# Middle of a 2-D FFT's row transform, woven into matmuls: its groups ordered by pairs of column halves

## The chip, the cores and the metric

The kernel runs on one core of a Trainium2 chip. The time is that of one execution on the device in microseconds (us); the median of several runs counts. The engines are TensorE (PE; its weight loads are shown as PEld), VectorE (DVE), ScalarE (ACT), GpSimd (POOL) and SyncE (SP). Each works through its own queue in order, and they wait for each other by semaphores. Transfers are issued by the queues of SP, ACT and POOL.

## The reference, cut to what is computed

```python
x = A_x                                              # 2048 x 1024, bf16
g = sigmoid((x * gate_w).sum(-1, keepdims=True))
a = irfft2(rfft2(x) * (w_r + 1j * w_i))              # over both axes, Df = 513
r = relu(B_x @ w1 + b1); b = (r * r) @ w2 + b2       # 1024 -> 3584 -> 1024
out = g * a + (1 - g) * b
# returned: out, and the gradients for A_x, w_r, w_i, w1, b1, w2, b2, gate_w
```

The gradients need the same transform of the incoming gradient, the product of both spectra (for w_r and w_i), and the way back.

## The kernel before, in words

**Main and side work.** The MLP is the main work: long chains of 128x128 matmuls on PE. First come `units` (`mlp_in`, up to about 456 us: chains `ph`, `pZ` and `pd`, four or eight matmuls each, L783 and L884), then `grads` (`mlp_grads`: `pX`, `pV`, L1206, up to about 850 us), then the outputs. The Fourier part is side work: generators that yield after each step. `spread` takes a number of side steps, given by a rate, between two pieces of the main work: 1.5 per piece while the middle of the transform runs beside `units` (one and two in turn; a unit is four pieces), 1.2 per piece beside `grads`, where most pieces count half, and from `res1` on what is left over 44 pieces (`todo`, L1870). So the Fourier part lies between main chains on every engine.

**Who sets the order.** The program's text gives the priority. A planner with estimated times then orders each engine's queue, and an instruction that it takes to be ready earlier may overtake. `behind` and `after(..., NoSync)` pin an order by hand. A tile is a buffer with a tag; `bufs` says how many such buffers there are, and whoever writes one anew waits for its last reader. In main work the wait that matters is on PSUM banks: ACT copies `cu` and `u` (L888), ACT's Relu (L898) and DVE's sum `rT` (L900) must have read a bank before PE goes on in it.

**The middle of the row transform** (`fft_mid`). The 2048 rows are 32 x 64. The first stage has left, for each of the 32 outputs c of a 32-point transform, 64 rows of complex numbers, for x and for the gradient, in `z_scr`. The middle takes c and 16 + c together as m = 0..15 (`NM`), and the columns in two halves: first h = 1, then h = 0. A pair of halves belongs to one m. For each (m, h), 32 in all:

- `inputs`: z is loaded (two transfers; from the third on issued by ACT, L404);
- `mirrored` (L425, m > 0): DVE makes pm, the sum and the difference of z's two parts;
- `transform`: px, four matmuls of 128 x 64 (L435), two for each half of the partitions, into a PSUM tile of tag `ps2`; ACT casts it into x (L436), writes a negated part (L437) and the edges (L438);
- `by_groups`: POOL lays out the filter w; `filters` (POOL's DMAs) loads filter and matrices of the next m;
- `products` (DVE, tt, two of L446) and `joined` (y, L451, L454, L458; eh by ACT, L455, L456): the filtered spectrum;
- `back`: pv, four matmuls of 64 x 128 (L466), into the other tile of `ps2`; ACT copies half of it (vc, L471), DVE makes pc (L472, L473), POOL stores it to `y_scr` (L475);
- `grads_of_w` (DVE, g and gs, L485, L486; g shares a buffer with tt) and `grads_out` (ACT, gw, L490, L495; POOL stores, L499): the gradient of the filter.

`ps2` has two buffers, so two tiles of px or pv are in use at a time. In the kernel before, the 32 halves are turns of four steps: step 1 px of this half and its x; step 2 pm of the next half, then pv and pc of the half before, then tt; step 3 y; step 4 gw of the half before, g and gs of this one. So px of one half and pv of another alternate, one step apart, at 4 steps a half.

`fft_out`, the last stage, loads `y_scr` after the middle has ended and begins its work 14 steps later.

Of the kernel before, what the change touches and what calls it, by code (L numbers as in the profile page):

```python
# [10 lines left out]
P = 128  # L11
BF16 = mybir.dt.bfloat16
FP16 = mybir.dt.float16
FP32 = mybir.dt.float32
ALU = mybir.AluOpType
ACT = mybir.ActivationFunctionType

FDT = FP16
# [123 lines left out]
def kernel(  # L142
# [22 lines left out]
    nc = tc.nc  # L165
# [8 lines left out]
    R1, R2 = g.R1, g.R2  # L174
    NT = S // P
    Q, H, LW, W1 = D // 4, D // 2, g.Df + 1, g.Df
# [8 lines left out]
    V, mm = nc.vector.tensor_tensor, nc.tensor.matmul  # L185
# [15 lines left out]
    pers, _ = pool("pers", stack=ctx)  # L201
    dram, _ = pool("dram", space=DRAM, stack=ctx)
# [25 lines left out]
    HW, HL = H // 2, P // 2  # L228
# [31 lines left out]
    def behind(ins, eng):  # L260
        after(ins, ahead[eng], mybir.DependencyClass.NoSync)
# [71 lines left out]
    def fft_mid(filler):  # L333
# [15 lines left out]

        def edges_through(ams):  # L350
            flat = lambda t_: t_[:].rearrange("p a b l -> p (a b l)")
            parted = fb.tile([P, 2, 2, HW], FDT, name="parted", tag="pm")
            parted = flat(parted)[:, 0 : 4 * P].rearrange("p (e k i) -> p e k i", e=4, i=NT)
            of_edge = edge[:].rearrange("p x t i -> p (x t) i").unsqueeze(2).to_broadcast([P, 4, 8, NT])
            of_part = part_of[:].unsqueeze(1).unsqueeze(3).to_broadcast([P, 4, 8, NT])
            tied = lambda ins: after(ins, later["last"], mybir.DependencyClass.NoSync)
            tied(V(out=parted, in0=of_edge, in1=of_part, op=ALU.mult))
            pe = fps.tile([P, 4, R1], FP32, name="pe", tag="ps2", bufs=2)
            for e in range(4):
                mm(pe[:, e, :], lhsT=parted[:, e].rearrange("p k i -> p (k i)"), rhs=row_of[:], start=True, stop=True, skip_group_check=True)  # L360
            ed = fb.tile([P, 2, 2, HW], FDT, name="ed", tag="y")
            ed = flat(ed)[:, 0 : NM * 8].rearrange("p (m n e) -> p m n e", n=2, e=4)
            by_row = pe[:].rearrange("p e c -> p c e")
            nc.vector.memset(ed[lanes[1], 0], 0.0)
            for n in range(2):
                tied(nc.vector.tensor_copy(out=ed[lanes[0], n:, n, :], in_=by_row[lanes[0], n:NM]))
                a, b = slice(2 * n, 2 * n + 2), slice(2 - 2 * n, 4 - 2 * n)
                tied(nc.vector.tensor_copy(out=ed[lanes[1], 1:, n, a], in_=by_row[lanes[1], NM + 1 :, a]))
                tied(nc.vector.tensor_scalar(out=ed[lanes[1], 1:, n, b], in0=by_row[lanes[1], NM + 1 :, b], scalar1=-1.0, scalar2=None, op0=ALU.mult))
            tied(nc.vector.tensor_copy(out=ed[lanes[0], 0, 1, :], in_=by_row[lanes[0], NM]))  # L370
            sp = fps.tile([P, NM, 2, 4], FP32, name="sp", tag="ps2", bufs=2)
            for h in range(2):
                for m in range(NM // 2):
                    for n in range(2):
                        mm(
                            sp[:, h * NM // 2 + m, n], lhsT=ams[h][:, m, n, :], rhs=ed[:, h * NM // 2 + m, n, :],
                            start=True, stop=True, skip_group_check=True,
                        )
            ex = fb.tile([P, NM, 3, 2, 2], FDT, name="ex", tag="ex")
            for n in range(2):  # L380
                for c in range(2):
                    nc.vector.tensor_copy(
                        out=ex[lanes[n], :, 1 + c], in_=sp[lanes[c], :, n, :].rearrange("p m (e t) -> p m t e", e=2)
                    )
            nc.scalar.mul(out=ex[:, :, 0], in_=ex[:, :, 2], mul=-1.0)
            return ex
# [32 lines left out]
        def mirrored(m, z, summed=None):  # L419

            if m == 0:
                return z
            pm = fb.tile([P, 2, 2, HW], FDT, name="pm", tag="pm")
            for n, op in enumerate((ALU.add, ALU.subtract)):
                mixed = V(out=pm[:, n], in0=z[:, 0], in1=z[:, 1], op=op)  # L425
                behind(mixed, "DVE")
                after(mixed, summed, mybir.DependencyClass.NoSync)
            return pm

        def transform(m, h, pm, ex):  # L430
            x = fb.tile([P, 3, 2, WL], FDT, name="x", tag="x", bufs=2)
            px = fps.tile([P, 2, 2, HW], FP32, name="px", tag="ps2", bufs=2)
            for c in range(2):
                for n in range(2):
                    behind(mm(px[lanes[n], c], lhsT=mats[m][:, 0, n, lanes[c]], rhs=pm[:, n], start=True, stop=True), "PE")  # L435
            nc.scalar.copy(out=x[:, 1:3, :, 0:HW], in_=px[:])  # L436
            copied = nc.scalar.mul(out=x[:, 0, :, 0:HW], in_=px[:, 1], mul=-1.0)  # L437
            nc.scalar.copy(out=x[:, :, :, h * HW], in_=ex[:, m, :, :, h])  # L438
            return x, copied
# [7 lines left out]
            return tt  # L447

        def joined(h, tt, eh):
            y = fb.tile([P, 2, 2, HW], FDT, name="y", tag="y")  # L450
            V(out=y[:], in0=tt[:, 0, :, :, 0:HW], in1=tt[:, 1, :, :, 0:HW], op=ALU.add)  # L451
            if h:
                en = fb.tile([P, 2, 2], FDT, name="en", tag="en")
                V(out=en[:], in0=tt[:, 0, :, :, HW], in1=tt[:, 1, :, :, HW], op=ALU.add)  # L454
                nc.scalar.mul(out=eh[:, 0], in_=en[:, 1], mul=-1.0)  # L455
                nc.scalar.copy(out=eh[:, 1], in_=en[:, 0])  # L456
            else:
                V(out=y[:, :, :, 0], in0=y[:, :, :, 0], in1=eh[:], op=ALU.add)  # L458
            return y

        def back(m, h, y):
            pc = fb.tile([P, 2, 2, HW], FDT, name="pc", tag="pc", bufs=2)
            pv = fps.tile([P, 2, 2, HW], FP32, name="pv", tag="ps2", bufs=2)
            for c in range(2):
                for n in (1, 0):
                    mm(pv[:, n], lhsT=mats[m][lanes[n], 1, c, :], rhs=y[lanes[n], c], start=c == 0, stop=c == 1)  # L466
            if m == 0:
                done = nc.scalar.copy(out=pc[:], in_=pv[:])
            else:
                vc = fb.tile([P, 2, HW], FP32, name="vc", tag="vc")  # L470
                done = nc.scalar.copy(out=vc[:], in_=pv[:, 1])  # L471
                V(out=pc[:, 0], in0=pv[:, 0], in1=vc[:], op=ALU.add)  # L472
                V(out=pc[:, 1], in0=pv[:, 0], in1=vc[:], op=ALU.subtract)  # L473
            for n, c in enumerate((m, R1 // 2 + m)):
                st(out=columns_of(y_scr, c, h), in_=pc[:, n])  # L475
            return done

        def grads_of_w(h, x):
            W = HW + h
# [20 lines left out]

        wn = {0: filters(0)}
        ams = [some_am(0), some_am(1)]
        turns = [(m, h) for m in range(NM) for h in (1, 0)]
        z = {0: inputs(*turns[0])}
        later["mid"] = True
        for _ in range(7):
            next(filler, None)
# [1 line left out]
        ex = edges_through(ams)  # L509
        for _ in filler:  # L510
            yield
        pm, w = mirrored(0, z.pop(0)), by_groups(1, wn[0])
        held = eh = gw = summed = None
        z[1] = inputs(*turns[1])
        yield
        for u, (m, h) in enumerate(turns):
            if h:
                eh = fb.tile([P, 2, 2], FDT, name="eh", tag="eh")
            x, copied = transform(m, h, pm, ex)
            if u + 2 < len(turns):  # L520
                z[u + 2] = inputs(*turns[u + 2], copied)
            yield
            if u + 1 < len(turns):
                pm = mirrored(turns[u + 1][0], z.pop(u + 1), summed)
            if held:
                done = back(*turns[u - 1], held)
            tt = products(h, x, w)
            if u + 1 < len(turns):
                m2, h2 = turns[u + 1]
                w = by_groups(h2, wn[m2])  # L530
            yield
            held = joined(h, tt, eh)
            yield
            if u:
                grads_out(*turns[u - 1], gs, gw, done)
            gs, summed = grads_of_w(h, x)
            if h:
                gw = fb.tile([P, 2, LW], BF16, name="gw", tag="gw", bufs=2)
                if m + 1 < NM:
                    wn[m + 1] = filters(m + 1)  # L540
            yield
        done = back(*turns[-1], held)
        grads_out(*turns[-1], gs, gw, done)
        yield
        fbs.close()

    def fft_out():
# [1319 lines left out]
        pass  # L1867
    grads = mlp_grads()
    next(grads), next(grads)
    todo = 4 * NT - 11 + 7 + 4 * R1 + 2 + 14 + 4 * NT  # L1870

    def rate():
        if "res1" not in later:
# [44 lines left out]
```

## Time and profile before

| | us |
|---|---|
| median of 3 runs | 1196.31 |
| lowest, highest | 1195.17, 1196.74 |
| the profiled execution, its own time | 1203.86 |
| its span, first to last instruction | 1202.1 |
| PE busy in the span | 1179.5 |
| px and pv first and last seen | 232.3, 596.0 |

The profile shows one execution. Busy time is the sum of what an engine worked; an idle time is put down to what released the engine. The lines are those of kernel.py. Matmuls are pipelined: one of 512 columns is shown as 0.38 us long, while the next starts 0.216 us after it, so their starts tell more than their lengths. Rows of the timeline merge neighbouring instructions of a kind (`x4`); their columns are start, extent, engine, line, operation, tile, array shape and operands. A row of the waits has the total, the number of times and the longest.

### The profile page before, as it was taken

How to read it: one execution, taken by the hardware profiler on the slowest of the kernel's cores; microseconds unless marked ns; L12 is line 12 of the kernel's file. 1: busy time of each engine (PE TensorE's matmuls, PEld its weight loads, DVE VectorE, ACT ScalarE, POOL GpSimd, SP SyncE). 2: the span in 40 equal slices, each digit the busy share in tenths (PEclk: the TensorE clock that was granted, in tenths of full speed). 3: DMA queues.
4: the chain of work that ended last, by engine and by line, in shares of the span. 5: the costliest groups of instructions: out<-in, count | busy, mean ns of one | idle time of the engine just before them, and what ended most of it. 6: DMA issues, size and time to landing. Idle time of an engine off the chain costs nothing.

```text
span 1202.1 us, 19429 instructions
## 1 busy us (share of the span) xinstructions
PE 1179.5 (98%) x7181; PEld 636.1 (53%) x7275; DVE 893.5 (74%) x1598; ACT 535.8 (45%) x961; POOL 375.9 (31%) x618
## 2 busy tenths in 40 slices
PE   8989999999999999999999999999999999999998
PEld 5555555443333444444446899999544444444444
DVE  5878887689898887776637666666786677986757
ACT  5657888576767783444414556564201010000000
POOL 0224433665666663553322322321001100000000
PEclk9999999999999999999999999999999999999999
DMA  9998585686969888989897999994889999665530
GB/s 242 295 237 244 179 210 185 203 200 192 220 189 212 246 243 174 206 183 220 202 225 141 232 218 249 252 208 151 258 170 251 270 255 280 192 188 153 179 123 36
DMA packets 329464, 249.84 MB, mean 208 GB/s; under 512 B 187912, under 2 KB 287658, under 8 KB 328858
## 3 DMA queue, kind: packets, MB, share of 16 engines
q1 hardware_dynamic: 268352, 112.12, 44.8%
q0 software_dynamic: 35136, 111.72, 29.4%
q10 hardware_dynamic: 25882, 24.76, 7.3%
q8 instruction: 57, 0.93, 0.3%
q14 instruction: 37, 0.30, 0.1%
HBM read 114.82 MB, written 89.67 MB: 170 GB/s over the span
## 4 chain that ended last, share of the span: by engine, by line
PE 73%; DVE 12%; DMA 5%; ACT 4%; issue 4%; SPq 1%; POOL 0%; ACTq 0%; another core or an unknown queue 0%; DVEq 0%; POOLq 0%
PE pX L1206 15%; PE xX L1505 13%; PE pV L1206 11%; PE pd L783 8%; PE xV L1505 6%; PE ph L884 6%; PE xZ L1505 3%; DMA dhT_scr<-dhT 1%; PE pui L325 1%; DVE rT L900 1%; PE ph L776 1%; PE pki L591 1%; PE px L435 1%; DVE dhT L787 1%; DMA z<-z_scr 1%
## 5 line engine op out<-in xcount | busy, mean ns | idle before, releaser
L783 PE MATMUL pd<-dbT,w2T 128*128 128x512 bf16 x859 | 205.4, 379 | 4.4 <-DMA w2T<-in_B_w_dram 2.0
L783 PEld LDWEIGHTS <-w2T 128*128 128x128 bf16 x896 | 86.3, 98 | 106.4 <-issue 3.9
L1505 PEld LDWEIGHTS <-dS 128*128 128x128 f16 x686 | 66.3, 98 | 79.1 <-issue 3.4
L787 DVE SCALAR_TENSOR_TENSOR dhT<-pd,rT 128x512 bf16<-128x512 f32 x112 | 76.6, 684 | 32.7 <-PE pd L783 26.0
L1556 POOL DMA_DIRECT2D out_dram<-ot x32 | 17.3, 542 | 249.4 <-DVE ot L1612 128.0
L1622 ACT ACTIVATE w2br<-w2br,dsc 128x512 f32<-128x512 bf16 x8 | 5.8, 722 | 175.0 <-DVE ot L1612 117.4
L1222 ACT COPY u<-pX 128x512 f32<-128x512 f32 x56 | 32.8, 585 | 98.7 <-PE pX L1206 92.6
L1505 PE MATMUL xX<-oT,dS 128*128 128x512 f16 x336 | 76.5, 379 | 0.2 <-DVE eR L1534 0.2
L1505 PEld LDWEIGHTS <-odd 128*128 128x128 bf16 (+1 forms) x462 | 44.8, 98 | 51.5 <-issue 0.9
L1505 PEld LDWEIGHTS <-even 128*128 128x128 bf16 (+1 forms) x448 | 43.6, 98 | 52.6 <-issue 0.7
L1206 PEld LDWEIGHTS <-T 128*128 128x128 f16 x672 | 64.7, 98 | 7.9 <-issue 0.7
L901 ACT ACTIVATE rT<-rT 128x512 bf16<-128x512 bf16 x69 | 43.3, 628 | 40.7 <-DVE rT L900 40.7
L751 ACT ACTIVATE h2T<-rT 128x1024 bf16<-128x1024 bf16 x56 | 59.7, 1065 | 0.5 <-issue 0.2
L1226 DVE TENSOR_TENSOR whi<-pV,u 128x512 bf16<-128x512 f32 x28 | 19.3, 690 | 51.6 <-ACT u L1222 48.1
L475 POOL DMA_DIRECT2D y_scr<-pc x64 | 46.9, 734 | 34.4 <-DVE pc L472 31.9
L446 DVE TENSOR_TENSOR tt<-x,w 128x1028 f16<-128x1028 f16 (+1 forms) x64 | 41.9, 691 | 17.0 <-issue 12.5
L1206 PEld LDWEIGHTS <-S 128*128 128x128 f16 x336 | 32.3, 98 | 41.0 <-DVE S L1138 1.3
L1206 PEld LDWEIGHTS <-resL 128*128 128x128 bf16 x448 | 43.0, 98 | 4.7
L1206 PEld LDWEIGHTS <-resR 128*128 128x128 f16 (+1 forms) x448 | 42.9, 98 | 4.9 <-issue 0.2
L1206 PEld LDWEIGHTS <-even 128*128 128x128 bf16 (+1 forms) x256 | 24.5, 98 | 30.8 <-issue 2.1
L815 POOL DMA_DIRECT2D h2T_scr<-h2T x28 | 20.7, 738 | 62.1 <-ACT f L285 30.8
L499 POOL DMA_DIRECT2D out_dram<-gw x64 | 34.4, 543 | 17.8 <-ACT gw L495 13.9
(381 smaller groups left out, 2757.8 us busy)
## 6 DMA issues: line engine op xcount, KB each, us to landing
h2T_scr<-h2T POOLq DMA_DIRECT2D x28, 512.0 KB, 4.4
dhT_scr<-dhT POOLq DMA_DIRECT2D x28, 512.0 KB, 5.2
y_scr<-pc POOLq DMA_DIRECT2D x64, 128.0 KB, 3.9
ax_scr<-yo POOLq DMA_DIRECT2D x16, 512.0 KB, 5.4
out_dram<-ot POOLq DMA_DIRECT2D x31, 256.0 KB, 3.1
z<-z_scr ACTq DMA_DIRECT2D x60, 128.0 KB, 4.4
out_dram<-whi POOLq DMA_DIRECT2D x28, 256.0 KB, 5.3
out_dram<-wlo POOLq DMA_DIRECT2D x28, 256.0 KB, 5.2
```

Source lines behind the costliest of these rows:

```text
L446: V(out=tt[:, k, :, :, 0:W], in0=x[:, a : a + 2, :, 0:W], in1=by, op=ALU.mult)
L475: st(out=columns_of(y_scr, c, h), in_=pc[:, n])
L499: st(out=every(dst_w, k), in_=gw[lanes[n], c_, 0:W1])
L751: after(nc.scalar.activation(h2T, rT, ACT.Square), behind_, mybir.DependencyClass.NoSync)
L783: mm(pd[:], lhsT=w_[:, ec, fc % FGC * P : (fc % FGC + 1) * P], rhs=dbT[:, ec, ss], start=(ec == 0), stop=(ec == DC - 1),)
L787: return STT(out=dhT, in0=pd[:], scalar=2.0, in1=rT, op0=ALU.mult, op1=ALU.mult, accum_out=gb1part[:, fc, sb : sb + 1],)
L815: st(out=scr[2 * fp : 2 * fp + 2, :, cols2].rearrange("c p s -> p c s"), in_=t_[:])
L884: mm(acc[:], lhsT=lhs[:, t, :], rhs=rhs[:, t, :], start=start and t == 0, stop=t == KH - 1, skip_group_check=True)
L901: nc.scalar.activation(rT, rT, ACT.Relu)
L1206: self.mm = mm(out, lhsT=lhs[:, t, m * P : (m + 1) * P], rhs=rhs[:, t, :], start=start and t + a == 0, stop=t == KH - 1, skip_group_check= ...
L1222: turn["ACT"] = nc.scalar.copy(out=t_[:], in_=self.X[:])
L1505: ins = mm(acc, lhsT=lhs[:, fc, :], rhs=rhs[:, fc, :], start=start and fc == 0, stop=fc == KH - 1 and bias is None, skip_group_check=True,)
```

## The change

The turns become a loop over m with eight steps, in which the two halves go together. `transform` is cut in two (`spectra`: px; `transform`: x), `back` in three (`rows_of`: pv; `copy_of`: vc; `back`: pc and its store). The steps of one m:

1. px of both halves; g and gs of the second half of m - 1; x of the first half; both z loads for m + 1
2. x of the second half
3. tt of the first half; gw of m - 1, both halves, and its stores; filter layout of the second half
4. pv of both halves of m - 1, vc of the first; filters of m + 1
5. y of the first half; pc of m - 1, first half
6. g and gs of the first half; pm of m + 1, first half; vc of m - 1, second half
7. pm of m + 1, second half; pc of m - 1, second half
8. tt and y of the second half; filter layout for m + 1, first half

(The first half is h = 1, the second h = 0.) From px of a half to its pv that is eleven steps instead of five. After the loop follow five steps instead of one, and `todo` grows by 4. pm becomes two tiles of half the size, the difference is written into z itself; y gets a second buffer, gw loses one. No instruction of the transform is added or taken away.

```diff
-            pm = fb.tile([P, 2, 2, HW], FDT, name="pm", tag="pm")
-            for n, op in enumerate((ALU.add, ALU.subtract)):
-                mixed = V(out=pm[:, n], in0=z[:, 0], in1=z[:, 1], op=op)
+            pm = fb.tile([P, 2, HW], FDT, name="pm", tag="pm", bufs=2)
+            for out, op in ((pm[:], ALU.add), (z[:, 1], ALU.subtract)):
+                mixed = V(out=out, in0=z[:, 0], in1=z[:, 1], op=op)
...
+        def spectra(m, pm):
             px = fps.tile([P, 2, 2, HW], FP32, name="px", tag="ps2", bufs=2)
             for c in range(2):
                 for n in range(2):
-                    behind(mm(px[lanes[n], c], lhsT=mats[m][:, 0, n, lanes[c]], rhs=pm[:, n], start=True, stop=True), "PE")
+                    behind(mm(px[lanes[n], c], lhsT=mats[m][:, 0, n, lanes[c]], rhs=pm[n], start=True, stop=True), "PE")
+            return px
...
-            y = fb.tile([P, 2, 2, HW], FDT, name="y", tag="y")
+            y = fb.tile([P, 2, 2, HW], FDT, name="y", tag="y", bufs=2)
...
-        for u, (m, h) in enumerate(turns):
-            if h:
-                eh = fb.tile([P, 2, 2], FDT, name="eh", tag="eh")
-            x, copied = transform(m, h, pm, ex)
-            if u + 2 < len(turns):
-                z[u + 2] = inputs(*turns[u + 2], copied)
-            yield
-            if u + 1 < len(turns):
-                pm = mirrored(turns[u + 1][0], z.pop(u + 1), summed)
-            if held:
-                done = back(*turns[u - 1], held)
-            tt = products(h, x, w)
-            if u + 1 < len(turns):
-                m2, h2 = turns[u + 1]
-                w = by_groups(h2, wn[m2])
-            yield
-            held = joined(h, tt, eh)
-            yield
-            if u:
-                grads_out(*turns[u - 1], gs, gw, done)
-            gs, summed = grads_of_w(h, x)
-            if h:
-                gw = fb.tile([P, 2, LW], BF16, name="gw", tag="gw", bufs=2)
-                if m + 1 < NM:
-                    wn[m + 1] = filters(m + 1)
-            yield
...
+        for m in range(NM):
+            more = m + 1 < NM
+            px = {h: spectra(m, pm[h]) for h in (1, 0)}
+            if m:
+                gs[0], _ = grads_of_w(0, x[0])
+            x[1], copied = transform(m, 1, px[1], ex)
+            if more:
+                z = {h: inputs(m + 1, h, copied) for h in (1, 0)}
+            yield
+            x[0], done = transform(m, 0, px[0], ex)
+            yield
+            tt = products(1, x[1], w[1])
+            if m:
+                gw = fb.tile([P, 2, LW], BF16, name="gw", tag="gw")
+                for h in (1, 0):
+                    grads_out(m - 1, h, gs[h], gw, done)
+            w[0] = by_groups(0, wn[m])
+            yield
+            if m:
+                pv = {h: rows_of(m - 1, y[h]) for h in (1, 0)}
+                vc = copy_of(m - 1, pv[1])
+            if more:
+                wn[m + 1] = filters(m + 1)
+            yield
+            eh = fb.tile([P, 2, 2], FDT, name="eh", tag="eh")
+            y[1] = joined(1, tt, eh)
+            if m:
+                back(m - 1, 1, pv[1], vc)
+            yield
+            gs[1], summed = grads_of_w(1, x[1])
+            if more:
+                pm = {1: mirrored(m + 1, z[1], summed)}
+            if m:
+                vc = copy_of(m - 1, pv[0])
+            yield
+            if more:
+                pm[0] = mirrored(m + 1, z[0])
+            if m:
+                back(m - 1, 0, pv[0], vc)
+            yield
+            tt = products(0, x[0], w[0])
+            y[0] = joined(0, tt, eh)
+            if more:
+                w[1] = by_groups(1, wn[m + 1])
+            yield
+        gs[0], _ = grads_of_w(0, x[0])
         yield
+        gw = fb.tile([P, 2, LW], BF16, name="gw", tag="gw")
+        for h in (1, 0):
+            pv = rows_of(NM - 1, y[h])
+            vc = copy_of(NM - 1, pv)
+            yield
+            back(NM - 1, h, pv, vc)
+            grads_out(NM - 1, h, gs[h], gw, vc[1])
+            yield
...
-    todo = 4 * NT - 11 + 7 + 4 * R1 + 2 + 14 + 4 * NT
+    todo = 4 * NT - 11 + 7 + 4 * R1 + 6 + 14 + 4 * NT
```

More of the change, by code (lines that the diff above doesn't have):

```diff
@@ L351, in edges_through @@
             flat = lambda t_: t_[:].rearrange("p a b l -> p (a b l)")
-            parted = fb.tile([P, 2, 2, HW], FDT, name="parted", tag="pm")
-            parted = flat(parted)[:, 0 : 4 * P].rearrange("p (e k i) -> p e k i", e=4, i=NT)
+            parted = fb.tile([P, 2, HW], FDT, name="parted", tag="pm", bufs=2)
+            parted = parted[:].rearrange("p b l -> p (b l)")[:, 0 : 4 * P].rearrange("p (e k i) -> p e k i", e=4, i=NT)
             of_edge = edge[:].rearrange("p x t i -> p (x t) i").unsqueeze(2).to_broadcast([P, 4, 8, NT])
@@ L360, in edges_through @@
                 mm(pe[:, e, :], lhsT=parted[:, e].rearrange("p k i -> p (k i)"), rhs=row_of[:], start=True, stop=True, skip_group_check=True)
-            ed = fb.tile([P, 2, 2, HW], FDT, name="ed", tag="y")
+            ed = fb.tile([P, 2, 2, HW], FDT, name="ed", tag="y", bufs=2)
             ed = flat(ed)[:, 0 : NM * 8].rearrange("p (m n e) -> p m n e", n=2, e=4)
@@ L421, in mirrored @@
             if m == 0:
-                return z
-            pm = fb.tile([P, 2, 2, HW], FDT, name="pm", tag="pm")
-            for n, op in enumerate((ALU.add, ALU.subtract)):
-                mixed = V(out=pm[:, n], in0=z[:, 0], in1=z[:, 1], op=op)
+                return z[:, 0], z[:, 1]
+            pm = fb.tile([P, 2, HW], FDT, name="pm", tag="pm", bufs=2)
+            for out, op in ((pm[:], ALU.add), (z[:, 1], ALU.subtract)):
+                mixed = V(out=out, in0=z[:, 0], in1=z[:, 1], op=op)
                 behind(mixed, "DVE")
                 after(mixed, summed, mybir.DependencyClass.NoSync)
-            return pm
-        def transform(m, h, pm, ex):
-            x = fb.tile([P, 3, 2, WL], FDT, name="x", tag="x", bufs=2)
+            return pm[:], z[:, 1]
+        def spectra(m, pm):
             px = fps.tile([P, 2, 2, HW], FP32, name="px", tag="ps2", bufs=2)
@@ L434, in transform @@
                 for n in range(2):
-                    behind(mm(px[lanes[n], c], lhsT=mats[m][:, 0, n, lanes[c]], rhs=pm[:, n], start=True, stop=True), "PE")
+                    behind(mm(px[lanes[n], c], lhsT=mats[m][:, 0, n, lanes[c]], rhs=pm[n], start=True, stop=True), "PE")
+            return px
+        def transform(m, h, px, ex):
+            x = fb.tile([P, 3, 2, WL], FDT, name="x", tag="x", bufs=2)
             nc.scalar.copy(out=x[:, 1:3, :, 0:HW], in_=px[:])
@@ L459, in joined, with rows_of @@
             return y
-        def back(m, h, y):
-            pc = fb.tile([P, 2, 2, HW], FDT, name="pc", tag="pc", bufs=2)
+        def rows_of(m, y):
             pv = fps.tile([P, 2, 2, HW], FP32, name="pv", tag="ps2", bufs=2)
@@ L466, in back, with copy_of @@
                     mm(pv[:, n], lhsT=mats[m][lanes[n], 1, c, :], rhs=y[lanes[n], c], start=c == 0, stop=c == 1)
+            return pv
+        def copy_of(m, pv):
             if m == 0:
-                done = nc.scalar.copy(out=pc[:], in_=pv[:])
-            else:
[L470 to L473, printed above, removed]
+                return None, None
+            vc = fb.tile([P, 2, HW], FP32, name="vc", tag="vc")
+            return vc, nc.scalar.copy(out=vc[:], in_=pv[:, 1])
+        def back(m, h, pv, vc):
+            pc = fb.tile([P, 2, 2, HW], FDT, name="pc", tag="pc", bufs=2)
+            if m == 0:
+                nc.scalar.copy(out=pc[:], in_=pv[:])
+            else:
+                V(out=pc[:, 0], in0=pv[:, 0], in1=vc[0][:], op=ALU.add)
+                V(out=pc[:, 1], in0=pv[:, 0], in1=vc[0][:], op=ALU.subtract)
             for n, c in enumerate((m, R1 // 2 + m)):
                 st(out=columns_of(y_scr, c, h), in_=pc[:, n])
-            return done
         def grads_of_w(h, x):
@@ L502, in fft_mid @@
         ams = [some_am(0), some_am(1)]
-        turns = [(m, h) for m in range(NM) for h in (1, 0)]
-        z = {0: inputs(*turns[0])}
+        z = {1: inputs(0, 1)}
         later["mid"] = True
@@ L511, in fft_mid @@
             yield
-        pm, w = mirrored(0, z.pop(0)), by_groups(1, wn[0])
-        held = eh = gw = summed = None
-        z[1] = inputs(*turns[1])
+        w = {1: by_groups(1, wn[0])}
+        z[0] = inputs(0, 0)
+        pm = {h: mirrored(0, z[h]) for h in (1, 0)}
+        x, y, gs, was = {}, {}, {}, None
         yield
-        for u, (m, h) in enumerate(turns):
-            if h:
-                eh = fb.tile([P, 2, 2], FDT, name="eh", tag="eh")
-            x, copied = transform(m, h, pm, ex)
-            if u + 2 < len(turns):
-                z[u + 2] = inputs(*turns[u + 2], copied)
-            yield
-            if u + 1 < len(turns):
-                pm = mirrored(turns[u + 1][0], z.pop(u + 1), summed)
-            if held:
-                done = back(*turns[u - 1], held)
-            tt = products(h, x, w)
-            if u + 1 < len(turns):
-                m2, h2 = turns[u + 1]
-                w = by_groups(h2, wn[m2])
-            yield
-            held = joined(h, tt, eh)
-            yield
-            if u:
-                grads_out(*turns[u - 1], gs, gw, done)
-            gs, summed = grads_of_w(h, x)
-            if h:
-                gw = fb.tile([P, 2, LW], BF16, name="gw", tag="gw", bufs=2)
-                if m + 1 < NM:
-                    wn[m + 1] = filters(m + 1)
-            yield
@@ L542, in fft_mid @@
-        done = back(*turns[-1], held)
-        grads_out(*turns[-1], gs, gw, done)
-        yield
+        for m in range(NM):
[6 more added lines that the diff above has]
+                z = {h: inputs(m + 1, h, copied) for h in (1, 0)}
+            yield
+            x[0], done = transform(m, 0, px[0], ex)
+            yield
+            tt = products(1, x[1], w[1])
[4 more added lines that the diff above has]
+            w[0] = by_groups(0, wn[m])
+            yield
+            if m:
[3 more added lines that the diff above has]
+                wn[m + 1] = filters(m + 1)
+            yield
+            eh = fb.tile([P, 2, 2], FDT, name="eh", tag="eh")
[19 more added lines that the diff above has]
+            yield
```

## The prediction

> **What bounds the kernel now.** I read the page first, then busy times by stretch, then TensorE's (PE's) waits and its timeline inside the stretch that the change touches: the first px matmul stands at 232.3 us, the last pv at 595.8. From the page, busy time and the chain that ended last:
>
> ```profile
> PE 1179.5 (98%) x7181; PEld 636.1 (53%) x7275; DVE 893.5 (74%) x1598; ACT 535.8 (45%) x961; POOL 375.9 (31%) x618
> ...
> PE 73%; DVE 12%; DMA 5%; ACT 4%; issue 4%; SPq 1%; POOL 0%; ACTq 0%; another core or an unknown queue 0%; DVEq 0%; POOLq 0%
> ```
>
> Busy time by stretch (PE, PEld, DVE, ACT, POOL, then granted clock, DMA share, GB/s):
>
> ```profile
> 228.00:456.00 228.00, 224.76 (x1098) 91.57 (x1118) 197.28 (x428) 165.34 (x289) 147.88 (x230) 1.00 0.81 210
> 456.00:600.00 144.00, 142.89 (x675) 60.20 (x684) 106.32 (x166) 61.49 (x113) 60.48 (x97) 1.00 0.90 200
> ```
>
> PE is the bound, before, in and after these stretches. VectorE (DVE) is second: 197.28 of 228, 87%, in the first stretch. What PE waited for between 228 and 600:
>
> ```profile
> PE ph L884 <- DVE rT L900: 1.4, 3, 0.5
> PE pd L783 <- DVE dhT L787: 0.4, 1, 0.4
> PE ph L884 <- ACT u L888: 0.2, 1, 0.2
> PE pV L1206 <- issue: 0.2, 1, 0.2
> ```
>
> Almost nothing, and no row names px or pv. Busy time hides a wait's first part, since matmuls overlap; from start to start I count 13 waits, 3.6 us together. So only PE's own time can be gained here. The timeline of PE shows some that does no work:
>
> ```profile
> 291.23 1.03 PE L884 MATMUL pZ<-xT,w1g 128*128 128x512 bf16 x4
> 292.19 0.62 PE L435 MATMUL px<-pm,ab 128*64 128x512 f16 x4
> 292.75 1.04 PE L884 MATMUL ph<-xT,w1g 128*128 128x512 bf16 x4
> 293.62 1.89 PE L783 MATMUL pd<-dbT,w2T 128*128 128x512 bf16 x8
> 295.35 1.03 PE L884 MATMUL ph<-dbn,Sw 128*128 128x512 f16 x4
> 296.31 0.60 PE L466 MATMUL pv<-y,ab 64*128 64x512 f16 x4
> 296.84 1.04 PE L884 MATMUL ph<-dbn,Sw 128*128 128x512 f16 x4
> 297.72 1.89 PE L783 MATMUL pd<-dbT,w2T 128*128 128x512 bf16 x7
> ...
> 300.47 1.89 PE L783 MATMUL pd<-dbT,w2T 128*128 128x512 bf16 x8
> 302.29 0.62 PE L435 MATMUL px<-pm,ab 128*64 128x512 f16 x4
> 302.85 0.61 PE L466 MATMUL pv<-y,ab 64*128 64x512 f16 x4
> 303.38 1.90 PE L783 MATMUL pd<-dbT,w2T 128*128 128x512 bf16 x8
> ```
>
> Read the starts. Eight plain matmuls (128*128) take 295.35 - 293.62 = 1.73 us, 0.216 each. Four from 291.23 should end with a next start at 292.10; px starts at 292.19, 0.09 late. Each change of array shape costs about that, into px, out of it, and likewise around pv.
>
> **The change part by part.**
>
> 1. *Adjacent groups.* A px group alone: from 291.23 to 293.62 are 2.39 us with eight plain matmuls (1.73) in them, so px costs 0.66. Its four matmuls run as two pairs; the group's extent 0.62 less one matmul (0.38, the shortest of the px rows) gives 0.24 per pair step. Eight in one run then cost 0.66 + 2 x 0.24 = 1.14 instead of 1.32: 0.18 saved. pv alone: 295.35 to 297.72 is 2.37, less 1.73: 0.64; pair step 0.60 - 0.38 = 0.22; eight in one run 1.08 instead of 1.28: 0.20 saved. But in 9 of the 32 halves px and pv already stand together, as at 302.29: 300.47 to 303.38 is 2.91, less 1.73, and 0.01 more in the next run: 1.19 instead of 1.30, and that 0.11 is lost again, since pv comes three steps after px. One px group (236.46 and 242.08) is now split, 0.2. Sum: 16 x 0.18 + 15 x 0.20 - 9 x 0.11 + 0.2 = **5.1 us saved**; the last pair's two pv groups stay apart. All of it is on PE, which nothing hides.
>
> 2. *The same work elsewhere.* Counts and shapes on DVE, ACT and POOL stay; the subtraction written into z is the same 0.42 us row. So nothing is gained or paid in busy time; the question is what is late next. A pair of halves takes 20.6 us in the first stretch (px at 281.39, 302.29, 322.95) for eight steps: 2.6 us a step; in the second about 26, 3.2 a step.
>
> 3. *Waits that get tighter.* (a) x of the second half is written by ACT in step 2 and needs its old contents read by DVE in step 1 (g and gs, 0.69 + 0.43); before, four steps lay between. Behind that cast on ACT stand copies cu and u (L888, 0.58) and the Relu of L898, and PE's next chain on the same bank waits for those; between the chain that makes u and the one that needs it lies one pd run, 1.73 us, so a copy may be 1.73 - 0.58 = 1.1 us late for nothing. (b) ACT's work comes in lumps: two x sets of 1.01 + 0.60 + 0.22 with four z loads issued between them (0.37 each, ACT's queue), then two gw sets in step 3 (2 x 1.12 + 2 x 0.21). With two steps between the same main pieces, ACT has 3.7 to 4.5 us at once, before at most 1.8 + 1.3. (c) DVE: steps 5 to 8 hold 2.3, 2.0, 2.2 and 2.4 us (y 0.81, en 0.16, pc 2 x 0.68, g and gs, pm 2 x 0.42, tt 2 x 0.69, the small y 0.24), steps 1 and 3 only 1.1 and 1.4, steps 2 and 4 nothing. The main work takes one or two steps in turn between two of its pieces, so three neighbouring pieces get up to 10.0 us, before 9.3. Against this, far more is ready at any time (pm, z and y stand two to seven steps ahead of their readers), and the planner fills idle DVE and ACT time with what is ready: DVE idled 17 us before tt alone (L446). The trace of before has no such wait, so I bound it. Below: all 3.6 us of today's waits go. Above: 1 us per pair in the 11.5 pairs of the first stretch, 11.5 us. I take **+1 us**, near the DVE waits seen (0.44 to 0.50 in the rows, three of them): a few more of that kind.
>
> 4. *Costs put at nothing.* gw in one buffer: its stores land in 5.3 us (9.3 the longest), the next writing is eight steps later. z: still five steps between load and pm, landing 4.4 us median, 11.7 the longest, now seen twice per pair; a late one would cost up to what exceeds 13 us. z's old contents are now released by px on PE, just ahead of the load. Filters: their DMAs on POOL come right behind the pv pair whose matrices they replace; POOL already waits so (ab, 11.6 us in 5), with y_scr, h2T and dhT stores behind it, each with a second buffer and a unit of 15 us before it is needed. y_scr stores: same 64, 3.9 us to land, spread over steps 5 and 7. Four more steps at the end: the row transform's inverse starts some 6 us later, but its pace is computed from what is left over 44 pieces, and PE has other work until 848 us: nothing, at most the four steps' DVE lag.
>
> Sum: the profiled execution took 1203.86 us (span 1202.1), 7.5 above the median of the runs, 1196.31. PE ran at clock 0.999 in it, so the saving carries over unscaled: 1196.3 - 5.1 + 1.0 = **1192.2 us**.
>
> A rule of the Trainium skill speaks against the change: "Perfetto Trace Analysis", section "Optimizing Tensor Performance", says that independent matmul groups should rotate through PSUM banks, so that emptying one overlaps the next group. What it would make here is rival D below.
>
> **The rivals.**
> - A, the forecast: 5.1 saved, waits about as now. For it: the switch costs are the same to 0.01 us wherever I looked, and PE never waited for px. 1192.2, from 1190 to 1193.8. Chance 0.50.
> - B, more work ahead also ends the waits for DVE: 1196.3 - 5.1 - 3.6 = 1187.6, to 1190. For it: DVE's idle time before tt. Chance 0.12.
> - C, the change doesn't do all it says: the order on PE is planned by estimated times, so main matmuls may fall between the two groups (it split a px group at 236.46), each split giving 0.2 back; half of them split and 2 us of new waits: 1196.3 - 2.5 + 2 = 1195.8. Or three or four lumps of (b) eat it. Chance 0.18.
> - D, slower: the cast of the second x holds ACT's queue, because DVE's step 8 (2.4) and step 1 (1.1) come just before, on an engine 87% full; cu and u are late and PE waits. It decides once a copy is over 1.1 us late; at 1 us of PE time per pair in 11.5 pairs: 1196.3 - 5.1 + 11.5 = 1202.7; it beats the saving from 0.45 us per pair. Against it: ACT is 73% busy there. Chance 0.15. Its second form: both buffers of ps2 are full after a px pair, and pv waits until both are empty, 2 x 1.61 us later if ACT is free; pv is due three steps, 7.7 us, behind, so ACT would have to be 4.5 us late; at 1 us in 15 pairs, 1206. Chance 0.05. (That is the skill's rule; no run here shows it yet.)
>
> 0.2%, about what a measurement of this kernel can tell from no change, is 2.4 us. Faster by more: A and B, 0.62; within: C, 0.18; slower: D, 0.20. The range goes from B's end, 1187.5, to 1201.5, which leaves out half of D and a little at the bottom.
>
> **What would show it.** In the changed profile's PE timeline, px rows of x8 with an extent of about 1.10 and pv rows of x8 of about 1.05, 16 and 15 times, alone between plain runs; a distance of about 2.87 us over px x8 and eight plain matmuls. PE's waits between 228 and 600 still 2 to 3 us (B: under 1; D: over 8, with ACT x, cu or u as releaser, or "PE pv" waiting for ACT x). The last pv about 4 to 8 us from 595.8. Wrong would be: rows of x4 (C), or a gain inside the stretch that a later one gives back by waiting for DMA, whose share is 0.93 between 600 and 850.

## The result, and the profile after

The changed kernel takes **1211.65 us** (median of 4 runs, 1210.24 to 1212.21); the kernel before took 1195.76 in the same job (4 runs). The ratio is 1.0130, with a 95% interval of 1.0113 to 1.0148: 15.9 us slower, where 4 us faster had been forecast.

The page of the changed kernel, busy time and the chain that ended last:

```profile
PE 1176.1 (97%) x7181; PEld 639.9 (53%) x7275; DVE 892.5 (74%) x1598; ACT 528.5 (44%) x961; POOL 377.6 (31%) x618
...
PE 69%; DVE 14%; ACT 6%; DMA 5%; issue 4%; POOL 1%; ACTq 1%; another core or an unknown queue 0%; SPq 0%; DVEq 0%; POOLq 0%
PE pX L1241 15%; PE xX L1540 13%; PE pV L1241 11%; PE pd L818 7%; PE xV L1540 6%; PE ph L919 5%; PE xZ L1540 3%; DMA out_dram<-gw 3%; PE pui L325 1%; DMA dhT_scr<-dhT 1%; DVE dhT L822 1%; PE pki L626 1%; ACT gw L499 1%; DVE rT L935 1%; PE pu L325 1%
```

PE's own busy time fell by 3.4 us, as it should when shapes change less often; its share of the chain fell from 73% to 69%. New in the chain is a transfer: the stores of gw, `out_dram<-gw`, with 3%, and the writing of gw on ACT behind it.

Where the time is shows by stretches with the same work in them. The profiled execution before had lost some us ahead of the change already: its first px came at 232.3 us, that of after at 226.0, from the same code. From the first px to the first pX (the first stretch), a row of before and one of after (the stretch, its length, busy time of PE, PEld, DVE, ACT and POOL with their instructions, the granted clock, the DMA share, GB/s):

```profile
232.30:466.40 234.10, 230.54 (x1093) 93.90 (x1115) 200.75 (x430) 169.00 (x296) 153.40 (x239) 1.00 0.81 210
```

```profile
226.00:473.80 247.80, 229.74 (x1092) 97.23 (x1113) 196.33 (x424) 164.49 (x296) 148.97 (x234) 0.99 0.77 198
```

So 13.7 us are lost here, with no engine busier but PE's weight loads (93.9 to 97.2 us) and the DMA share lower. From the first pX to the first output chain it is 381.9 us before and 382.1 after, and 353.8 and 354.2 from there to the end; the last 2 us or so of the 15.9 cannot be placed from one profile of each. PE's four largest waits in the first stretch of after (total, times, longest), 15.1 us together:

```profile
PE pd L818 <- DVE dhT L822: 5.3, 5, 2.1
PE ph L919 <- ACT rT L933: 4.7, 2, 2.7
PE ph L919 <- ACT cu L923: 3.1, 2, 1.9
PE ph L919 <- ACT u L923: 2.0, 2, 1.2
```

All its waits there were 2.0 us before. From start to start I count 19.3 us here, 3.5 before: 15.8 more. Against it, px and pv change the array's shape 47 times instead of 84 in this stretch, 4.8 instead of 8.6 us. One half-speed spell of PE adds 1.7 us (last section): 15.8 - 3.8 + 1.7 = 13.7.

What held ACT, in its own waits of after:

```profile
ACT gw L504 <- DMA out_dram<-gw: 32.1, 12, 4.2
```

Before, no wait of gw for its stores is there at all. And so it looks in the timeline, one of the twelve: ACT, then POOL, then PE.

```profile
296.59 0.22 ACT L441 COPY x<-ex 128x6 f16<-128x6 f16 x1
297.44 0.63 ACT L936 ACTIVATE rT<-rT 128x512 bf16<-128x512 bf16 x1 [0.63 <-DVE rT L935]
302.11 0.21 ACT L504 ACTIVATE gw<-gs 128x2 bf16<-128x2 f16 x1 [4.05 <-DMA out_dram<-gw]
302.22 0.57 ACT L475 COPY vc<-pv 128x512 f32<-128x512 f32 x1
302.69 0.69 ACT L933 ACTIVATE rT<-ph,b1col 128x512 bf16<-128x512 f32 x1
```

```profile
294.91 2.10 POOL L508 DMA_DIRECT2D out_dram<-gw  x4 [0.98 <-ACT gw L504]
```

```profile
299.94 0.81 PE L919 MATMUL pZ<-xT,w1g 128*128 128x512 bf16 x3
303.43 1.02 PE L919 MATMUL ph<-xT,w1g 128*128 128x512 bf16 x4 [2.68 <-ACT rT L933]
```

POOL issues gw's four stores from 294.91 to 297.01. The write of gw that stands next in ACT's queue is L504: two columns of the *next* pair, 0.21 us long. It waits for the last store, until 302.11. Behind it stands the Relu that empties the bank PE needs, and PE waits 2.68 us. PE's row names the Relu, ACT's row names the store: only both together give the cause.

Each half's gw is written by two instructions, a large one (L499) and the small one (L504). `grads_out` pins the large one behind a copy of x or vc. The small one is not pinned; it needs only gs, which DVE makes in step 6, and for the first half it touches other columns than the large one. So it was put ahead, to where the stores of the one buffer had just been issued. In the case above DVE's gs was ready at 294.98, while the stores were being issued from 294.91 on:

```profile
294.55 0.43 DVE L495 TENSOR_TENSOR gs<-g 128x514 f16<-128x514 f16 x1
```

### The profile page after: what moved, and what is told of

Same layout as the page of the kernel before. It is cut to its first block, busy times and chain, and to the rows that moved or that the text cites. A ratio compares the mean times of both kernels' runs of the same rounds, so it can differ in the third digit from the quotient of the medians.

```text
span 1210.1 us, 19414 instructions
## 1 busy us (share of the span) xinstructions
PE 1176.1 (97%) x7181; PEld 639.9 (53%) x7275; DVE 892.5 (74%) x1598; ACT 528.5 (44%) x961; POOL 377.6 (31%) x618
## 4 chain that ended last, share of the span: by engine, by line
PE 69%; DVE 14%; ACT 6%; DMA 5%; issue 4%; POOL 1%; ACTq 1%; another core or an unknown queue 0%; SPq 0%; DVEq 0%; POOLq 0%
PE pX L1241 15%; PE xX L1540 13%; PE pV L1241 11%; PE pd L818 7%; PE xV L1540 6%; PE ph L919 5%; PE xZ L1540 3%; DMA out_dram<-gw 3%; PE pui L325 1%; DMA dhT_scr<-dhT 1%; DVE dhT L822 1%; PE pki L626 1%; ACT gw L499 1%; DVE rT L935 1%; PE pu L325 1%
## 5 line engine op out<-in xcount | busy, mean ns | idle before, releaser
L818 PE MATMUL pd<-dbT,w2T 128*128 128x512 bf16 x860 | 208.4, 380 | 7.5 <-DVE dhT L822 5.3
L1261 DVE TENSOR_TENSOR whi<-pV,u 128x512 bf16<-128x512 f32 x28 | 19.3, 689 | 48.4 <-ACT u L1257 48.3
L1261 DVE TENSOR_TENSOR wlo<-pV,u 128x512 bf16<-128x512 f32 x28 | 19.2, 686 | 34.4 <-PE pV L1241 34.2
L919 PEld LDWEIGHTS <-w1g 128*128 128x128 bf16 x252 | 23.9, 98 | 37.8 <-issue 11.9
```

The lines of the kernel that those rows point to most:

```text
L818: mm(pd[:], lhsT=w_[:, ec, fc % FGC * P : (fc % FGC + 1) * P], rhs=dbT[:, ec, ss], start=(ec == 0), stop=(ec == DC - 1),)
L919: mm(acc[:], lhsT=lhs[:, t, :], rhs=rhs[:, t, :], start=start and t == 0, stop=t == KH - 1, skip_group_check=True)
L1261: turn["DVE"] = self.added = V(out=self.half(row, j), in0=self.sums(acc), in1=self.sums(t_), op=ALU.add)
```

## The experiments

Theory **G**: the one buffer of gw together with this small write holds ACT's queue. Rival **L**: the pair order makes lumps of work on ACT and DVE that hold PE, whoever is named. All times are medians, all ratios against the kernel before on the same chip.

**e2, the small write pinned**, one buffer as in the change:

```diff
-            nc.scalar.mul(out=gw[:, :, h * H], in_=gs[:, :, h * HW], mul=0.5 * GS)
+            edge_ = nc.scalar.mul(out=gw[:, :, h * H], in_=gs[:, :, h * HW], mul=0.5 * GS)
+            after(edge_, done, mybir.DependencyClass.NoSync)
```

> The changed kernel; the small write of gw (the two edge columns) may no longer overtake: it is pinned behind the same copy as the large write. gw keeps its one buffer. Theory G (ACT's queue is held by this write, which the planner has brought forward to where the stores of the last gw have not landed): ACT's idle time before gw that ends with the stores falls from 32.1 us in 12 times to under 3, PE's waits in the first stretch from 19 to 5 us or less, and the time is 1191 to 1199. Rival L (the lumps of ACT and DVE work that the pair order makes hold PE, whoever is named in the waits): PE still waits 12 us or more, 1204 to 1212.

1197.84 us, ratio 1.0005 (0.9984 to 1.0025). ACT never waits for gw's stores, and PE's waits in the first stretch are:

```profile
PE ph L920 <- ACT u L924: 3.5, 4, 1.3
PE pd L819 <- DVE dhT L823: 3.0, 3, 1.5
PE ph L920 <- DVE rT L936: 0.4, 1, 0.4
```

One pin takes back 14 us: G. But 6.9 us of waits are left (8.9 from start to start, 5.4 more than before), not 5 or less, and they cancel the 5.1 us that the shapes save.

**e3, the kernel before with one gw buffer:**

```diff
-                gw = fb.tile([P, 2, LW], BF16, name="gw", tag="gw", bufs=2)
+                gw = fb.tile([P, 2, LW], BF16, name="gw", tag="gw")
```

> The kernel before with one buffer for gw instead of two, nothing else. Theory G: the edge write of the next pair is ready one step after the stores of the last are issued here too, so ACT waits for them, 20 us or more in 8 times or more, and the time is 1201 to 1212. Rival L: without the pair order there are no lumps, and one buffer costs nothing: 1194 to 1198.

1226.62 us, ratio 1.0236 (1.0202 to 1.0271). In ACT's waits:

```profile
ACT gw L495 <- DMA out_dram<-gw: 50.6, 7, 12.1
...
ACT gw L490 <- DMA out_dram<-gw: 11.5, 5, 3.9
```

The loss comes without any pair order, and at 30.0 us it is larger than I had put it: G again, L out as the main cause.

**e4, e3 with the pin; e9, the kernel before with the pin and both buffers.**

> The kernel before with one buffer for gw (as in e3), and the edge write pinned behind the copy that the large write is pinned behind. Theory G: the pin alone takes back most of what the one buffer cost, 1226.6 to 1196 to 1204; ACT's wait for the stores falls from 62 us to under 12. Rival: in this order the large write waits as well, and it stays over 1212.

> The kernel before, both gw buffers, with the edge write pinned: a control. Theory G: with two buffers there is no wait for stores to take away, so within 0.2% of before, 1194 to 1199. Rival: the pin is a gain of its own in any order, 1192 or less, and then e2 says nothing on the buffer.

e9: 1196.08 us, ratio 1.0001 (0.9989 to 1.0013): the pin alone is worth nothing. e4: 1208.22, ratio 1.0098 (1.0083 to 1.0114), between the two expectations: the pin takes back 18.4 of the 30.0 us, less than I had put it, and the rival's number missed too. ACT's wait did fall from 62.1 to 10.2 us, but these are four waits of the large write of up to 4.2 us (in this order it comes four steps after the last), and PE still waited 9.4 us in three pieces for the Relu behind it. Two spells of PE at half clock, as described in the last section, add 3.4 us. The sum of ACT's waits does not give the cost: 10.2 us of them go with a loss of 11.6 us here, 32.1 us with one of about 14 in the changed kernel.

Two buffers for gw in the new order, the most direct test, were not tried; the change gave up gw's second buffer and gave y one, and no run shows whether both fit.

**What is left in e2.** Four edits of e2 look for it: pv of the second half moved to step 6 (e8), gw of the first half moved to step 7 of its own pair (e5), the second half's z loads moved to step 2 (e6), the last two together (e7).

```diff
-                pv = {h: rows_of(m - 1, y[h]) for h in (1, 0)}
+                pv = {1: rows_of(m - 1, y[1])}
...
+                pv[0] = rows_of(m - 1, y[0])
                 vc = copy_of(m - 1, pv[0])
```

> The pinned version (e2), but pv of the second half is issued two steps after pv of the first, so that 15 runs of eight pv become 30 of four. Theory: what adjacency saves is real, 0.20 us for each pv run, and is only hidden by the waits: 30 more changes of shape, PE's time for them up by 3.0 us, and the time up by 2 to 4 us against e2. Rival: the adjacent groups save nothing that counts, or pv apart evens out the lumps: within 1 us of e2 or faster.

```diff
...
-                gw = fb.tile([P, 2, LW], BF16, name="gw", tag="gw")
-                for h in (1, 0):
-                    grads_out(m - 1, h, gs[h], gw, done)
+                grads_out(m - 1, 0, gs[0], gw, done)
...
+            gw = fb.tile([P, 2, LW], BF16, name="gw", tag="gw")
+            grads_out(m, 1, gs[1], gw, vc[1] if m and vc[1] else done)
             yield
...
```

> The pinned version (e2), but gw of the first half is written in step 7 of its own pair instead of step 3 of the next, so that step 3 holds one gw set (1.3 us of ACT) and not two. Theory L2 (what is left of PE's waits, 8.9 us in the first stretch, comes from ACT's lump of x and two gw sets ahead of u, and from DVE's lumps): PE's waits for u, 3.5 us, fall to 1 or less, those for dhT (DVE) stay at about 3; time 2 to 3 us under e2. Rival: the waits for u only move to another copy, time within 1 us of e2.

```diff
-                z = {h: inputs(m + 1, h, copied) for h in (1, 0)}
+                z = {1: inputs(m + 1, 1, copied)}
...
             x[0], done = transform(m, 0, px[0], ex)
+            if more:
+                z[0] = inputs(m + 1, 0, done)
```

> The pinned version (e2), but the z loads of the second half are issued in step 2 behind its own x instead of in step 1, so that two and not four issues (0.4 to 0.5 us each) stand together in ACT's queue. Theory: the four issues hold cu by up to 1.1 us, but PE's waits name u and dhT, so this is worth little: within 1 us of e2. Rival: the issues are what delays u and, through rT, dhT: 2 us or more under e2.

> Both: gw of the first half in step 7, and the z loads apart. Theory L2: like e5 or up to 1 us better, 2 to 4 us under e2, so 0.1 to 0.3% under the kernel before. Rival: no better than e2.

| | us | ratio | what the trace shows |
|---|---|---|---|
| e8 | 1208.76 | 1.0106 (1.0088 to 1.0125) | 28 more changes of shape, 2.8 us; late z loads |
| e5 | 1208.59 | 1.0099 (1.0083 to 1.0115) | the large write of gw waits for stores, 18.5 us in 8; late z loads |
| e6 | 1200.91 | 1.0032 (1.0016 to 1.0048) | PE waits 4.9 for u; pm waits for z, 6.3 us in 4 |
| e7 | 1204.38 | 1.0052 (1.0038 to 1.0066) | gw's stores 9.5 us in 6 |

All four missed their numbers. e8 shows that adjacency is worth what the rows say (eight pv in one run keep PE for 1.07 us, in two runs of four for 1.27, and 14 runs were cut in two), but most of its 11 us over e2 come from elsewhere: in DVE's waits of e8

```profile
DVE pm L425 <- DMA z<-z_scr: 9.4, 2, 7.4
```

two z loads took 20.0 and 20.6 us to land, DVE stood, PE waited 5.7 us, and a spell at half clock lost another 3.4. Why these loads were late stays open. e5 brought back G's wait, now of the pinned write: four steps after the stores are too few. It shows once more what the one buffer does to ACT, and is no test of the lumps. e6, no faster than e2, speaks against the z issues as what delays u.

**e10, gw late**: the two gw sets in step 4 and step 5 instead of both in step 3.

```diff
-            if m:
-                gw = fb.tile([P, 2, LW], BF16, name="gw", tag="gw")
-                for h in (1, 0):
-                    grads_out(m - 1, h, gs[h], gw, done)
...
                 vc = copy_of(m - 1, pv[1])
+                gw = fb.tile([P, 2, LW], BF16, name="gw", tag="gw")
+                grads_out(m - 1, 1, gs[1], gw, done)
...
                 back(m - 1, 1, pv[1], vc)
+                grads_out(m - 1, 0, gs[0], gw, done)
```

> The pinned version (e2) with the two gw sets moved from step 3 to step 4 (first half, behind vc) and step 5 (second half), so that they stand apart from the x sets and 7 steps lie between the stores and the next write. Theory L2 (ACT's lump of x and two gw sets ahead of u makes PE wait 3.5 us): PE's waits for u, cu and the Relu under 2 us in the first stretch, waits for dhT as in e2; time 1 to 4 us under e2, 0 to 0.3% under before. Rival: another late wait takes its place, no better than e2.

1196.17 us, ratio 0.9993 (0.9980 to 1.0006). PE's waits in the first stretch:

```profile
PE pd L818 <- DVE dhT L822: 5.4, 6, 1.5
PE pd L818 <- DVE rT L935: 1.0, 1, 1.0
PE ph L811 <- ACT rT L933: 0.3, 1, 0.3
PE ph L919 <- ACT u L923: 0.2, 1, 0.2
```

The waits for u are gone, 3.5 to 0.2 us: ACT's lump was their cause. The sum is as large as in e2, though, 6.9 us, since the waits for dhT grew from 3.0 to 5.4, which was not expected, and the time cannot be told from e2's: the intervals overlap. In e2's DVE timeline one sees what stands ahead of a dhT that PE waits for:

```profile
287.26 0.68 DVE L494 TENSOR_TENSOR g<-x 128x1024 f16<-128x1024 f16 x1
287.97 0.42 DVE L495 TENSOR_TENSOR gs<-g 128x512 f16<-128x512 f16 x1
288.53 1.30 DVE L449 TENSOR_TENSOR tt<-x,w 128x1028 f16<-128x1028 f16 x2
289.87 0.17 DVE L457 TENSOR_TENSOR en<-tt 128x4 f16<-128x4 f16 x1
289.95 0.69 DVE L823 SCALAR_TENSOR_TENSOR dhT<-pd,rT 128x512 bf16<-128x512 f32 x1
```

**e12, e13, e14: side work on DVE pinned.** e12 is e10 with tt pinned behind the last dhT issued so far; e13 pins g and pm too; in e14 the pin is the last sum of the second stage, once there is one.

```diff
-                V(out=tt[:, k, :, :, 0:W], in0=x[:, a : a + 2, :, 0:W], in1=by, op=ALU.mult)
+                after(V(out=tt[:, k, :, :, 0:W], in0=x[:, a : a + 2, :, 0:W], in1=by, op=ALU.mult), later["last"], mybir.DependencyClass.NoSync)
```

> The version with late gw (e10), and tt may no longer overtake: it is pinned behind the last dhT that the text has issued ahead of it. Theory D (what is left of PE's waits, 8 us in the first stretch, comes from side work on DVE that the planner has put ahead of a dhT that PE waits for, tt above all): PE's waits for dhT fall from 5.4 us to 2.5 or less, time 1192 to 1195. Rival: the lump only moves behind dhT and delays rT and the Relu instead: within 1 us of e10.

> As e12, with g and pm pinned in the same way. Theory D: the waits for dhT at about 1 us, time 1190 to 1194, under the kernel before by 0.2 to 0.5%. Rival: pinned side work comes late for the matmuls of px and pv, and PE waits for them: 1197 or more.

> As e13, and beside the second stage of the main work the same side operations are pinned behind the last sum of that stage on DVE, because PE waits 2.1 us there for one such sum. Theory D: that wait falls under 1 us and the rest stays as in e13, 1192 to 1194.5, 0.1 to 0.4% under the kernel before. Rival: the pins hold side work behind sums of 2.3 us each and PE waits for px or pv: 1196 or more.

e12: 1197.47 us, ratio 1.0009 (1.0000 to 1.0018), not 1192 to 1195. The waits for dhT fell as expected, from 5.4 to 0.8 us, but waits for cu, rT and the Relu (3.2 us) came up, much as its rival said; from start to start the waits fell from 8.1 to 5.8 us in the profile, the time did not, and why stays open. e13: 1194.47, ratio 0.9990 (0.9978 to 1.0002), half a us above its range and not clear of no change. e14: **1192.66, ratio 0.9958 (0.9941 to 0.9976)**, faster than both kernels. Its first stretch, and PE's waits there:

```profile
225.00:455.30 230.30, 227.20 (x1092) 96.77 (x1113) 193.68 (x421) 165.69 (x294) 151.35 (x231) 1.00 0.80 212
```

```profile
PE ph L920 <- DVE rT L936: 0.8, 3, 0.5
PE ph L920 <- ACT rT L934: 0.5, 1, 0.5
PE pd L819 <- DVE dhT L823: 0.3, 1, 0.3
PE pv L469 <- ACT x L441: 0.2, 1, 0.2
PE pd L819 <- issue: 0.2, 1, 0.2
```

With the waits where they were before (2.0 us), the order by pairs gives 3.8 us in the first stretch (234.1 to 230.3), and 4.2 us in the medians (2.9 to 7.1 by the interval). The kernel before with the same pins on DVE was not run; that the gain is the shapes' and not the pins' is argued from the equal waits.

## Why the prediction was wrong, point by point

- **What bounds the kernel** was right: PE, and only PE's own time could be gained.
- **1, adjacent groups** was right. Around the first pair shown here, in after:

```profile
290.80 1.24 PE L818 MATMUL pd<-dbT,w2T 128*128 128x512 bf16 x5
291.97 1.04 PE L468 MATMUL pv<-y,ab 64*128 64x512 f16 x8
292.94 0.82 PE L818 MATMUL pd<-dbT,w2T 128*128 128x512 bf16 x3
```

  Five plain matmuls end at 291.88, pv starts 0.09 later and keeps PE until 292.94: 1.06 us for eight, 1.08 forecast. px of eight, counted in the same way (from 283.62, the next plain run at 284.61), costs 1.08, 1.14 forecast. There are 70 changes of shape in both stretches instead of 121, 51 x 0.1 = 5.1 us saved, as forecast. In part that is luck: 15 runs of eight px and 14 of pv came, one less of each than counted (px of the first pair stands apart too), and each px run was cheaper than forecast (its later pairs follow at 0.21 to 0.22 us, where I took 0.24).
- **2** was right: busy times stay or fall a little (DVE 893.5 to 892.5, ACT 535.8 to 528.5, POOL 375.9 to 377.6 us).
- **3, the tighter waits**: (b) and (c) were there and were sized too small. Without G they cost 8.9 - 3.5 = 5.4 us (e2), where I took +1; the profile of e10 shows (b) in the waits for u, those of e12 and e13 show (c) with tt, g and pm. Wait (a) is seen once in after, 2.1 us of ACT before a write into x (at 476.60), behind the first stretch.
- **4, costs put at nothing, is the step that failed**: "gw in one buffer: its stores land in 5.3 us (9.3 the longest), the next writing is eight steps later". The stores do land in 5.3 us. But I counted the steps of the text for the large write, and overlooked that gw is also written by a second, unpinned instruction, whose input is made in step 6, three steps of the text behind the stores and not eight. In the twelve waits that input was ready 0.1 to 7.4 us after the first of the stores was issued, at most about two steps. e2 puts this error at 1211.65 - 1197.84 = 13.8 us (14.7 if each is taken against the kernel before in its own job, 15.9 and 1.2 us above it).
- **The rivals**: D named the right queue and the right victims (cu, u and the Relu late on ACT, PE waiting over 8 us), but another cause, and its price, 1 us a pair, was under the 1.4 us (15.8 us more in 11.5 pairs) that came. C and B did not happen: beside the last pair's pv, which the text keeps apart, two groups are split, px of the first pair and pv of the pair at the end of the first stretch. Nor did PE wait for a full `ps2`, with pv three steps behind px: none of its waits in after names px or pv. The Trainium skill ("Perfetto Trace Analysis", "Optimizing Tensor Performance") says that independent matmul groups should rotate through PSUM banks, so that one is emptied during the next. Two groups on end in both buffers cost nothing measurable here; the most that pv waited for x in any version is 0.5 us (e12).
- **The sum** would have missed without the error in 4 as well: e2 is that kernel, and it stands 1.2 us above before (-1.9 to +3.0 by the interval), where 4.1 below were forecast, since 3 was 4.4 us short. e14, which takes away what 3 and 4 missed, stands 4.2 us under before. That this meets the 4.1 so closely bears out the saving of 1, not the forecast: e14 moves gw and pins work on DVE, which the change does not do.

## What to carry to other kernels

When a buffer is taken away, list *every* instruction that writes it, the smallest too, and ask for each how early its inputs allow it to stand in its queue; the distance in the text holds only for those that are pinned. An instruction of 0.2 us that waits 4 us holds all that stands behind it, so read a wait of the busy engine together with the waits of the engine that it names. And where an order is planned, look for what the planner puts ahead of what the bound engine waits for: here a gain of 4 us came out only once that side work was pinned.

## What the runs showed of the hardware

A wait of PE can cost more than its length. After the wait of 2.07 us at 356.32 in after, the granted clock was half for 3.4 us (1.00, 0.50, 1.00 in the rows):

```profile
350.00:356.60 6.60, 4.47 (x25) 1.85 (x21) 6.43 (x15) 3.49 (x5) 5.56 (x10) 1.00 0.39 111
356.60:360.00 3.40, 3.40 (x10) 1.16 (x9) 0.33 (x1) 3.21 (x7) 0.67 (x1) 0.50 1.18 211
360.00:366.00 6.00, 5.95 (x32) 2.44 (x32) 5.07 (x12) 3.92 (x11) 3.85 (x7) 1.00 0.56 131
```

Half speed for 3.4 us loses 1.7 us. e3 had four such spells and e4 two; e8 had one of 6.8 us that began near the end of its wait of 5.7. After the wait of 2.68 us at 303.43 there was none, so length alone does not decide it. The Trainium skill ("TensorE: Matmul & The Clock Gate", "Part 1: The HAM clock gate") says that the clock goes to half after PE has been idle for a window of about 3.4 us. A spell here is as long as such a window, 3.41 us, but waits of 2.07 us (after) and 2.2 us (e3) were followed by one, so as a limit on a single wait the rule does not hold here.
